# Block attention and routed experts on one core: another order of the steps of every attention pair

## The chip, the core and the metric

The kernel runs on one core of a Trainium2 chip. The metric is the device time of one execution in microseconds (us). It was timed three times before the change, and once more under the hardware profiler.

## What is computed

Eight batches of eight heads attend over 576 positions of width 64 with a mask by blocks of 64. The 4608 resulting rows of 512 then go through a layer of eight experts, each row through the one expert that its router picks.

```python
scores = scale * np.matmul(q, k.transpose(0, 1, 3, 2))          # (8, 8, 576, 576)
scores = np.where(block_i >= block_j, scores, -1000000000.0)
attn = np.exp(scores - np.max(scores, axis=-1, keepdims=True))
attn = attn / (np.sum(attn, axis=-1, keepdims=True) + 1e-09)
x = np.matmul(attn, v).transpose(0, 2, 1, 3).reshape(4608, 512)
...
logits = xn @ en.T / tau                                        # 8 experts
expert_idx = np.argmax(logits, axis=1)
...
    h = np.maximum(x[mask] @ w1[e], 0.0)
    out[mask] = gate_w[mask, None] * (h @ w2[e])
```

## The kernel before

Attention goes first, in 32 pairs of heads (four pairs to a batch), then the experts' layer in slots of 128 rows. The change touches the attention alone.

The work on a pair is cut into steps, Python generators that issue a few instructions and yield. Pass `n` of the loop over pairs (line 739) draws from five of them, which belong to different pairs, so that the engines always have work of several kinds:

- `s`, `scores` (line 377), pair n, ten steps, five to a head. TensorE (PE) forms a transposed tile of scores by two products (L384, L385) in one of two PSUM buffers `pss`; ScalarE (ACT) takes the exponential (L394, L401); GpSimd (POOL) adds tiles up for the sums of a row (L375). The second product reads `qx`, in which one row is the negated maxima of the pair.
- `v`, `values` (line 406), pair n-1, nine steps. Steps 1 to 6 are the products of the probabilities with v (L414): the two heads go to the two halves of PE's columns, in tiles of 128 by 64. Step 7 forms the sums with a matrix of ones (L423, L424, L428) in tiles of 128 by 32. Steps 8 and 9 copy sums and products out of PSUM, on VectorE (DVE, L430) and on ACT (L432). All of it lies in the one buffer `psb`.
- `f`, `post` and `finish` (line 437), pair n-1, four steps after the values: two of PE (L452, L456), turning the products into `psb` again, and two of DVE (L460 to L473), which read `psb` and divide.
- `m`, `maxes` (line 345), pair n+1, eleven steps: ten products of q and k on PE (L353), each in one of two buffers `psm` that DVE reduces to maxima (L355), then a turn of the maxima on PE (L360), a copy on ACT (L362), and two small DMAs (L364) that put them into `qx`.
- `p`, `prep` (line 297), pair n+2, six steps: turns of q (step 1) and of k (step 4) on PE (L312), copies on ACT (L324, L328, L333), the low parts by subtraction on DVE (L303, steps 2, 3, 5 and 6), a DMA of `qx` (L326) and four of `ka` (L336).

Two more letters stand in a plan. `l` loads q, k and v of pair n+3 (seven DMAs, L204 to L212; in pass 29 the first weights, L160). `r` draws one step of the router of the batch before (line 509): small DVE operations, six products for the ranks of its rows in `psm` (L538 to L542), the squares on ACT (L504), the store of the rows, and five scatters by indirect DMA on POOL (L604). Behind the last `r` of the batch before the last come the reading of a table (L630, a DMA of SyncE) and of the first rows for the experts (L499).

All DMAs but the scatters and gathers are issued by SyncE (SP), in the program's order. Every engine works its instructions in the order in which the program issues them, and waits by semaphores where an operand is not ready. So the order within a pass is set by one string of letters: eight of them stand in `PLANS` (line 21), number 0 to 7 here. Pass n takes plan n mod 4, the last four passes (28 to 31) plans 4 to 7; pass 0 has a plan of its own. A generator that is not drawn to its end by the string is drawn to it at the end of the pass.

```python
        for c in PLANS[n % NP + (NP if n >= NPAIR - NP else 0)] if n else PLAN0:   # line 744
            if c == "l":
                ...
            elif c != "r":
                parts[c] = drain(parts[c], 1)
            if c == "r" and slow and drain(slow[0], 1) is None:
                slow.pop(0)
```

Of the kernel before, what the change touches and what calls it, by code (L numbers as in the profile page):

```python
# [18 lines left out]


PLANS = (
    "vvrmmsvvmmsrrvrrpmsrmvvvsvmrmrsrsprmrrmrlpffssrrmrfmfrrpspsp",
    "vvmrrmrvrrvvrsmmrsvpsmrmvvsvmmspsmrfprmlfsmrfsfppprrssm",
    "rvvmmvvvrmrrmrrsrpvsrrsrmmvslvmvmpssmmfrrfrpffmssppmspsrrr",
    "vvvrmrrsrrrsrmrvrrrrrmmprrvsmmrrvvrsrrrvvmmrrrsspmmfrfrrmpslsprrrfrrrfrppssm",
    "vvvrsmmrvrrrvvrrmmrvvrrrrrssrmrlrrrmvrpsmrsmmrpfsrrrpfmrsfmmrsfpsrprprrs",
    "vvrvrrrmrrpmsrsrmpvvsrmlrrsrvvsvvrmrrsrmmrrrrfrrmsmpmfrmsffprmprrssp",
    "vvrrrrmrvvprvrrlmrsrvrrmsmrrrspvvmsspmvrrpsmfprrmmrsfrmmrsrrrsfpmrrsrfrrr",
    "mvrrvvprssvvpvmsrlrsmrrmrrmrrrvrvssvrssfmrfmmrprprmmpmpsfsfrm",
)  # L30
PLAN0 = "kmsmsmmsmmkpsmsspkmmmpmslsspspp"

# [1361 lines left out]
```

## Time and profile before

| | us |
|---|---|
| median of three runs | 895.87 (895.05 to 896.83) |
| the profiled execution, its own time | 888.07 |
| its span, from the first to the last instruction | 886.2 |
| end of the last exponential of pass 31, from the start of the span | 423.85 |

Attention takes the first half of the span, with passes of 12.4 to 12.7 us in the middle; the experts' layer takes the second half. A time in the rows below counts from the start of the span. A PE row names the stationary operand's tile (128*128, 128*64), and its end is modelled; the start of one product and of the next one tell how long PE was taken up by it.

### The profile page before, as it was taken

The page shows a single profiled execution, that of the slowest core. Times are in us where ns is not written, and L with a number is a line of the kernel's source. Part 1 is how long each engine was busy: PE and PEld are TensorE (multiplying, and loading weights), DVE is VectorE, ACT ScalarE, POOL GpSimd, SP SyncE. Part 2 cuts the span into 40 slices and gives each one's busy share as a digit, 9 for nine tenths or more (in the row PEclk, how much of TensorE's full clock was granted, in tenths as well). Part 3 has the DMA queues.
Part 4 walks back from the last instruction along what each step waited for, and adds up shares of the span by engine and source line. Part 5 has one row for each costly group of instructions (what it writes and reads, how often), then busy time and mean ns, then how long its engine had stood idle before and what let it go on. Part 6 is the DMA issues. An engine that isn't in the chain of part 4 may idle for free. (4 is left out here: it accounts for less than half of the span.)

```text
span 886.2 us, 18968 instructions
## 1 busy us (share of the span) xinstructions
PE 856.8 (97%) x5149; PEld 675.4 (76%) x5149; DVE 589.5 (67%) x1297; ACT 482.5 (54%) x959; POOL 522.0 (59%) x657
## 2 busy tenths in 40 slices
PE   5999999999999999998899999999899999999997
PEld 4777777777777777765687888888688888888885
DVE  8678888788888888784767534544667544566442
ACT  4655768576675767574745444645445333444331
POOL 6444664656555664648645322335688887687863
PEclk8899999999999999999999999999999999999999
DMA  8967877777887888774529443554676554354441
GB/s 157 190 153 148 172 179 162 171 152 169 170 188 149 165 185 162 165 190 139 190 79 301 140 144 130 172 208 164 215 242 205 187 171 155 119 159 140 151 134 48
DMA packets 172330, 146.67 MB, mean 166 GB/s; under 512 B 132009, under 2 KB 141449, under 8 KB 170652
## 3 DMA queue, kind: packets, MB, share of 16 engines
q1 hardware_dynamic: 150668, 100.14, 47.0%
q0 software_dynamic: 14896, 32.89, 12.3%
q10 hardware_dynamic: 6624, 12.06, 3.7%
q8 instruction: 51, 0.84, 0.4%
q14 instruction: 91, 0.75, 0.3%
HBM read 85.12 MB, written 31.79 MB: 132 GB/s over the span
## 5 line engine op out<-in xcount | busy, mean ns | idle before, releaser
L355 DVE TENSOR_REDUCE nmx<-psm 128x1 f32<-128x320 f32 x315 | 135.0, 452 | 46.3 <-PE psm L353 41.8
L394 ACT ACTIVATE pT<-pss 128x448 f32<-128x448 f32 (+1 forms) x254 | 112.6, 452 | 93.6 <-PE pss L385 88.7
L375 POOL TENSOR_TENSOR pS<-pT 128x448 f32<-128x448 f32 x64 | 72.9, 1139 | 128.7 <-ACT pT L394 128.7
L375 POOL TENSOR_TENSOR pS<-pS,pT 128x320 f32<-128x320 f32 (+2 forms) x192 | 115.6, 602 | 23.8 <-ACT pT L401 7.5
L384 PE MATMUL pss<-qb,ka 128*128 128x448 f32 (+1 forms) x382 | 126.4, 343 | 0.5 <-ACT pT L394 0.3
L1020 PE MATMUL py<-ring_h,hh 128*128 (+1 forms) x288 | 114.1, 396 | 2.6 <-ACT hh L964 2.3
L414 PE MATMUL psb<-pT,vo 128*64 128x448 f32 (+4 forms) x768 | 111.8, 408 | 1.7 <-DVE lgh L473 1.2
L1020 PE MATMUL py<-ring_h,hl 128*128 (+1 forms) x288 | 113.1, 393 | 0.2 <-DVE hl L962 0.2
L1020 PE MATMUL py<-ring_l,hh 128*128 (+1 forms) x288 | 112.7, 391 | 0.0
L385 PE MATMUL pss<-qx,kx 70*128 70x448 f32 (+1 forms) x382 | 109.3, 309 | 2.8 <-DMA qx<-nmT 2.8
L1020 PE MATMUL ph<-ring_h,xl 128*128 x280 | 109.3, 390 | 1.0 <-DVE xl L1013 1.0
L1020 PE MATMUL ph<-ring_h,xh 128*128 x280 | 110.0, 393 | 0.0
L1020 PE MATMUL ph<-ring_l,xh 128*128 x280 | 109.1, 390 | 0.0
L788 DVE TENSOR_TENSOR ring_l<-raw,ring_h 128x1024 f32 (+1 forms) x64 | 81.2, 1279 | 26.4 <-ACT ring_h L784 19.4
L1069 POOL DMA_INDIRECT out_dram<-y,outi x36 | 40.3, 1118 | 93.9 <-ACT y L1066 80.5
L353 PE MATMUL psm<-kd,qd 128*128 128x320 f32 x315 | 89.6, 347 | 3.1 <-ACT kd L333 1.8
L384 PEld LDWEIGHTS pss<-qb,ka 128*128 128x128 f32 x382 | 73.4, 192 | 21.6 <-issue 6.3
L1066 ACT ACTIVATE y<-py,gate 128x512 f32<-128x512 f32 x36 | 24.8, 689 | 116.8 <-PE py L1020 95.0
L353 PEld LDWEIGHTS psm<-kd,qd 128*128 128x128 f32 x315 | 55.5, 194 | 37.0 <-ACT pT L401 13.4
L1038 ACT ACTIVATE h<-ph 128x512 f32<-128x512 f32 x70 | 41.7, 598 | 76.7 <-PE ph L1020 69.0
L385 PEld LDWEIGHTS pss<-qx,kx 70*128 70x128 f32 x382 | 73.8, 193 | 4.0 <-DMA qx<-nmT 1.8
L784 ACT CAST ring_h<-raw 128x1024 f32 (+1 forms) x68 | 70.3, 1053 | 7.5 <-ACTq L929 4.2
(270 smaller groups left out, 1785.6 us busy)
## 6 DMA issues: line engine op xcount, KB each, us to landing
raw<-in_moe_w_dram SPq DMA_DIRECT2D x40, 512.0 KB
ka<-kd SPq DMA_DIRECT2D x128, 144.0 KB
raw<-in_moe_w_dram SPq DMA_DIRECT2D x12, 1024.0 KB
hrows<-h ACTq DMA_DIRECT2D x46, 256.0 KB
hq<-hrows POOLq DMA_DIRECT2D x92, 128.0 KB, 2.8
qn<-in_q_dram SPq DMA_DIRECT2D x64, 144.0 KB
kn<-in_k_dram SPq DMA_DIRECT2D x64, 144.0 KB
qx<-qb SPq DMA_DIRECT2D x32, 288.0 KB
```

What stands on the lines that cost most here:

```text
L353: nc.tensor.matmul(mx[:, 0:max(e - a, 256)], qd[d][:, j, :, :], kd[d][:, a:a + max(e - a, 256)], start=True, stop=True)
L355: nc.vector.tensor_reduce(m[:, j + u:j + u + 1], mx[:, 0:e - a], axis=AX.X, op=ALU.max, negate=True)
L375: nc.gpsimd.tensor_tensor(o, pT[0:r, P:S] if t == 1 else o, pT[0:r, off[t]:off[t] + w], op=ALU.add)
L384: nc.tensor.matmul(o, ka[i][:, hh, ts], qb[i][:, hh, c0:c1], start=True, stop=False)
L385: nc.tensor.matmul(o, kx[i][0:KX, hh, ts], qx[i][0:KX, hh, c0:c1], start=False, stop=True)
L394: nc.scalar.activation(pT[:, o:o + c1 - c0], st[:, 0:c1 - c0], AF.Exp, scale=scale)
L414: nc.tensor.matmul(ob[hh * D:(hh + 1) * D, c0:c1], a[:, t, hh, :], pTs[hh][0][:, o:o + c1 - c0], start=(t == 0), stop=(c0 == OB or t == NJ ...
L784: return nc.scalar.copy(piece(ring_h, to, c, half), raw[i][:, c * CW:(c + 1) * CW])
L788: return eng.tensor_tensor(piece(ring_l, to, c, half), raw[i][:, c * CW:(c + 1) * CW], piece(ring_h, to, c, half).bitcast(F32), op=ALU.sub ...
L1020: m = nc.tensor.matmul(out, a[:, c, :], w, start=(c == 0 and w is wh and a is sh), stop=(c == nk - 1 and a is sl_))
L1038: nc.scalar.activation(h[:, f:f + 512], ph, AF.Relu)
L1069: nc.gpsimd.indirect_dma_start(out=out, out_offset=bass.IndirectOffsetOnAxis(ap=to, axis=0), in_=y, in_offset=None, bounds_check=NT - 1, o ...
```

## The change

The eight strings of `PLANS` are replaced; nothing else. All letters but `r` stand in each new string as often as in the old one (`v` nine times, `s` ten, `m` twelve, `p` six, `f` four, `l` once); of `r` there are 18, 13, 16 and 34 in plans 0 to 3 before and 58, 11, 17 and 19 now, and 30, 26, 31 and 19 in plans 4 to 7 before and 34, 29, 24 and 19 now. The two most different of the first four:

```diff
 PLANS = (
-    "vvrmmsvvmmsrrvrrpmsrmvvvsvmrmrsrsprmrrmrlpffssrrmrfmfrrpspsp",
...
-    "rvvmmvvvrmrrmrrsrpvrsrrsrmmvslvmvmpssmmfrrfrpffmssppmspsrrr",
...
+    "vvvvvvlsrrmrmvvvrrrrrmrrsmsrpmrrsrrrrrrrmprrfmrrprrsmrrsrrrrffrmsrrrrsprrmrrrrrsrsrrrmrrrrrrmrrrfrpp",
...
+    "rrrmmrvrrrvrrvvrvrvvsrvvmmsplsmsmpfmmssprfmmrrffsspmmpssrrp",
...
 )
```

On PE, in a pass with plan 2, from the first product of the values on. Before:

```order
L414 MATMUL psb<-pT,vo_170 64x128 x2
L414 MATMUL psb<-pT,vo_170 64x448 x2
L353 MATMUL psm<-kd_200,qd_198 128x320
L353 MATMUL psm<-kd_200,qd_198 128x256
L414 MATMUL psb<-pT,vo_170 64x448 x2
L414 MATMUL psb<-pT,vo_170 64x320 x2
L414 MATMUL psb<-pT,vo_170 64x192 x2
L353 MATMUL psm<-kd_200,qd_198 128x512
L353 MATMUL psm<-kd_200,qd_198 128x448
L384 MATMUL pss<-qb_187,ka_193 128x288
L385 MATMUL pss<-qx_190,kx_196 128x288
L312 MATMUL pst<-ident,qn 128x96 x6
```

And now, at the same place:

```order
L353 MATMUL psm<-kd_200,qd_198 128x320
L353 MATMUL psm<-kd_200,qd_198 128x256
L414 MATMUL psb<-pT,vo_170 64x128 x2
L414 MATMUL psb<-pT,vo_170 64x448 x4
L414 MATMUL psb<-pT,vo_170 64x320 x2
L414 MATMUL psb<-pT,vo_170 64x192 x2
L414 MATMUL psb<-pT,vo_170 64x64 x2
L423 MATMUL psb<-pT,ones 32x128
L424 MATMUL psb<-pS,ones 32x320
```

The products of the values (L414) and of the sums (L423 to L428) stood in four pieces in this pass, with maxima, scores and turns between them; now they stand in one, with the first two products of the maxima ahead of it. A piece is counted from the first of these products to the next product of another kind. Over the whole attention there were 123 pieces and there are now 50: 4 for each of the values of pairs 0 to 26 before and 2, 1, 1, 2 in turn now (108 and 40 in all), and 15 and 10 for those of pairs 27 to 31.

On SP, in a pass with plan 2, up to the stores that follow it (`qx<-nmT` are the maxima, `ka<-kd` the turned k). Before:

```order
L326 DMA qx_190<-qb_187 64x1152
L364 DMA qx_189<-nmT 1x9x64 x2
L336 DMA ka_193<-kd_199 64x576 x4
L492 DMA xbuf<-xrow 64x256
L493 DMA xbuf<-xrow 128x4x256
```

and now:

```order
L326 DMA qx_190<-qb_187 64x1152
L336 DMA ka_193<-kd_199 64x576 x4
L364 DMA qx_189<-nmT 1x9x64 x2
L492 DMA xbuf<-xrow 64x256
L493 DMA xbuf<-xrow 128x4x256
```

The two DMAs of the maxima stood ahead of the four of `ka`, and stand behind them now. This is so in plans 0, 1 and 2; in plan 3 the maxima still go first.

On POOL, in pass 30, between the additions of pass 29 and the gather of the first rows. Before:

```order
L604 DMA table<-tokf,rowj 36864x1 x3
L375 TENSOR_TENSOR pS<-pT 128x448
L375 TENSOR_TENSOR pS<-pS,pT 128x320
L375 TENSOR_TENSOR pS<-pS,pT 128x192
L375 TENSOR_TENSOR pS<-pS,pT 64x64
L604 DMA table<-tokf,rowj 36864x1 x2
```

and now:

```order
L580 TENSOR_TENSOR ss<-ss,half 128x5
L604 DMA table<-tokf,rowj 36864x1 x5
L375 TENSOR_TENSOR pS<-pT 128x448
L375 TENSOR_TENSOR pS<-pS,pT 128x320
L375 TENSOR_TENSOR pS<-pS,pT 128x192
L375 TENSOR_TENSOR pS<-pS,pT 64x64
```

The last two scatters stood behind the additions of the pass's first head; now all five stand ahead of them. The reading of the table on SP (L630), which waits for the last scatter, stands ahead of the two DMAs of the maxima of pass 30 in both orders.

## Rows read from the trace of the kernel before

**Rows 1.** The page of the profile: the span, and the busy time of the engines over it.
```profile
span 886.2 us, 18968 instructions
PE 856.8 (97%) x5149; PEld 675.4 (76%) x5149; DVE 589.5 (67%) x1297; ACT 482.5 (54%) x959; POOL 522.0 (59%) x657
```

**Rows 2.** Busy time by stretch, passes 16, 17 and 18 of the loop over pairs one by one, then passes 20 to 23 together, then passes 28 to 31 together (a pass ends with its last exponential). Columns: start and end, length, and for PE, PE weight loads (PEld), DVE, ACT and POOL the busy time with the number of instructions; then the granted clock, the share of DMA time and GB/s.
```profile
219.05:231.53 12.48, 12.48 (x100) 9.23 (x96) 9.53 (x25) 7.67 (x17) 8.01 (x12) 1.00 1.00 198
231.53:244.00 12.47, 12.47 (x104) 9.58 (x102) 11.15 (x35) 7.79 (x18) 5.85 (x9) 1.00 0.72 145
244.00:256.37 12.37, 12.28 (x98) 9.49 (x96) 10.86 (x34) 11.34 (x28) 7.07 (x10) 1.00 0.77 162
...
269.03:318.99 49.96, 49.88 (x392) 37.68 (x390) 41.97 (x121) 34.73 (x79) 29.58 (x40) 1.00 0.81 167
...
368.95:423.85 54.90, 50.23 (x352) 34.65 (x348) 33.98 (x105) 31.55 (x88) 35.72 (x51) 0.97 0.67 176
```

**Rows 3.** Waits of PE alone between 60 and 400 us, the two longest of the three that there are. Columns: who waited, for whom, us in total, times, the longest.
```profile
PE psm L560 <- DVE accb L555: 0.6, 1, 0.6
PE psm L360 <- DVE nmx L355: 0.5, 1, 0.5
```

**Rows 4.** The timeline of PE in passes 17 to 19 (start us, duration us, line, tiles, shape, how many in a row). L414 is a product of the values, L384 and L385 one of the scores, L353 one of the row maxima, L312 a turn of q or k, L360 the turn of the maxima.
```profile
234.22 0.40 PE L384 MATMUL pss<-qb,ka 128*128 128x288 f32 x1
234.46 0.30 PE L385 MATMUL pss<-qx,kx 70*128 70x288 f32 x1
234.59 0.60 PE L353 MATMUL psm<-kd,qd 128*128 128x512 f32 x2
235.03 0.29 PE L384 MATMUL pss<-qb,ka 128*128 128x288 f32 x1
235.16 0.29 PE L385 MATMUL pss<-qx,kx 70*128 70x288 f32 x1
235.39 0.34 PE L414 MATMUL psb<-pT,vo 128*64 128x64 f32 x4
...
243.43 1.19 PE L414 MATMUL psb<-pT,vo 128*64 128x128 f32 x8
244.55 0.53 PE L353 MATMUL psm<-kd,qd 128*128 128x320 f32 x2
245.01 1.84 PE L414 MATMUL psb<-pT,vo 128*64 128x448 f32 x12
246.77 0.70 PE L353 MATMUL psm<-kd,qd 128*128 128x512 f32 x2
...
253.60 0.27 PE L360 MATMUL psm<-ident,nmx 128*9 128x128 f32 x1
255.95 1.94 PE L414 MATMUL psb<-pT,vo 128*64 128x128 f32 x12
257.82 0.41 PE L353 MATMUL psm<-kd,qd 128*128 128x320 f32 x1
258.20 0.30 PE L385 MATMUL pss<-qx,kx 70*128 70x288 f32 x1
...
258.81 0.76 PE L414 MATMUL psb<-pT,vo 128*64 128x320 f32 x4
259.50 0.70 PE L353 MATMUL psm<-kd,qd 128*128 128x512 f32 x2
...
260.63 0.55 PE L414 MATMUL psb<-pT,vo 128*64 128x192 f32 x4
261.11 0.47 PE L384 MATMUL pss<-qb,ka 128*128 128x448 f32 x1
```

**Rows 5.** The timeline of DVE in pass 14, from the last row maxima to the end of the division by the sums (L460 to L473).
```profile
202.57 0.42 DVE L355 TENSOR_REDUCE nmx<-psm 128x1 f32<-128x128 f32 x2
...
204.15 0.16 DVE L460 TENSOR_SCALAR rin<-psb 128x2 f32<-128x2 f32 x1
...
205.81 0.75 DVE L303 TENSOR_TENSOR kx<-pst,kd 64x576 fp32r<-64x576 f32 x1
```

**Rows 6.** SyncE's own timeline in pass 18: when it issued DMAs (start us, time that the issuing took, line, destination and source, how many).
```profile
254.19 1.58 SPq L364 DMA_DIRECT2D qx<-nmT  x2
255.88 2.69 SPq L336 DMA_DIRECT2D ka<-kd  x4
```

**Rows 7.** DMA issues of line L336 over the whole run: nanoseconds of one issue, least, median and most.
```profile
L336 SPq DMA_DIRECT2D ka<-kd x128: 469/587/2927, 8.2 to 399.3; - x128
```

**Rows 8.** Groups of instructions of ACT in passes 16 to 27, shapes kept apart: line, operation, tiles, shape, count, then busy us and mean ns of one, then the idle time before.
```profile
L333 ACT CAST kd<-pst 128x576 fp32r<-128x576 f32 x12 | 7.7, 640 | 0.0
```

**Rows 9.** The timeline of all engines at the end of pass 30 and the start of pass 31, by engine; what stands in brackets is how long the engine sat idle before, and what ended it.
```profile
408.50 0.26 ACT L362 CAST nmT<-psm 9x128 fp32r<-9x128 f32 x1 [0.79 <-PE psm L360]
...
411.62 0.34 SPq L630 DMA_DIRECT2D et<-table  x1
...
412.07 1.59 SPq L364 DMA_DIRECT2D qx<-nmT  x2
...
413.95 0.40 PE L385 MATMUL pss<-qx,kx 70*128 70x288 f32 x1 [1.59 <-DMA qx<-nmT]
```

**Rows 10.** Busy time by stretch at the same place, columns as in rows 2.
```profile
410.60:414.00 3.40, 1.81 (x10) 0.52 (x6) 0.00 (x0) 1.88 (x10) 3.08 (x6) 1.00 0.03 1
414.00:417.00 3.00, 3.00 (x16) 1.95 (x17) 0.00 (x0) 0.71 (x2) 1.80 (x5) 0.60 0.56 156
```

More of the change, by code (lines that the diff above doesn't have):

```diff
@@ L21 @@
 PLANS = (
-    "vvrmmsvvmmsrrvrrpmsrmvvvsvmrmrsrsprmrrmrlpffssrrmrfmfrrpspsp",
[L23 to L29, printed above, removed]
+    "vvvvvvlsrrmrmvvvrrrrrmrrsmsrpmrrsrrrrrrrmprrfmrrprrsmrrsrrrrffrmsrrrrsprrmrrrrrsrsrrrmrrrrrrmrrrfrpp",
+    "rrvvvrrvvvlmmvvvmmssprmsrmrsfpmmsfspmmsrpssrfrmrfppms",
+    "rrrmmrvrrrvrrvvrvrvvsrvvmmsplsmsmpfmmssprfmmrrffsspmmpssrrp",
+    "mmvvvvrvvvrrrvrvmrmssrprmrrlrrssrmrfprmmssrfpmmssrfmfppprrssm",
+    "vrvvvrmrmssmrrrrprmrsrrmsrvrvrvrprpvmsrslrvrrrmpmrrsmrsrppmrrrffssrrmrfrmrrf",
+    "prrmmvvrpvvrvprvmsrmvvsrvmrmsprsmlsrrrmsrrsfprrrrrrrsmmfrsmsfrmrrfprrrr",
+    "mmpppvvprrvvvvrvrrrssrvrmrppvlrrrrmrssmfrmmsrsmfrmrrmsrrsmsrfrrmfs",
+    "vvvvvrrrmrrssmrpvrrmmsrsrrprplmrvsmsvvmpmpprssrfrfmsmsrrmmrff",
 )
```

## The prediction

> **What bounds the kernel now.** I read the busy times by stretch first. In the middle of attention PE is busy in all but 0.08 us of 49.96 that four passes take, at the full clock; DVE is busy for 41.97 of them and ACT for 34.73 [rows 2]. The waits of PE say the same: from 60 to 400 us the longest two are 0.6 and 0.5 us in all [rows 3]. So from pass 1 to 27 PE never stands still, and a pass can become shorter only if PE's own work becomes shorter. The page's 97% for PE alone would not tell this [rows 1], since it also holds the experts' half.
>
> Next I read the timeline of PE, by the starts of its products [rows 4]. The same product takes more of PE's time when it stands beside a piece of the values' products. A second score product holds PE for 0.13 us ahead of an ordinary product (234.46 to 234.59) and for 0.23 ahead of a piece (235.16 to 235.39): entering costs 0.10. The first score product behind a piece holds it for 0.24 (234.22 to 234.46) and an ordinary one for 0.13 (235.03 to 235.16): 0.11. Within the pieces, steps 1 to 3 in one took 1.87 (255.95 to 257.82) and steps 1 and 2 took 1.12 (243.43 to 244.55), so step 3 inside a piece is 0.75. Steps 3 to 5 in one took 1.76 (245.01 to 246.77), so steps 4 and 5 inside one are 1.01. In pieces of their own they took 0.69 and 0.48 (258.81 to 259.50, 260.63 to 261.11), 0.16 more for the one piece more. So a piece costs 0.10 + 0.11 + 0.16 = **0.37 us** of PE. The tile of the stationary operand changes there, 128*128 to 128*64 and back.
>
> **The change, part by part.** Values' steps. The values of pairs 0 to 26 go from 108 pieces to 40: 68 x 0.37 = 25.2 us less of PE. Those of pairs 27 to 31 go from 15 to 10: 1.9 less. The amount of arithmetic is the same. Four passes of 49.96 would come down by 10 x 0.37 to 46.3.
>
> The Trainium skill ("TensorEngine Tiling", Key Properties) says that changing the tiling mode drains TensorE, and ("TensorE: Matmul & The Clock Gate", Single matmul latency) gives a warm product a fixed part of 398 cycles at 2.4 GHz. An estimate from that page is 0.17 us for each change and 0.33 for a piece; 73 pieces would then give 24.2 us instead of the 27.1 by the rows, which I keep.
>
> Cover. DVE, ACT and POOL hid under PE's 49.96; they must now fit 46.3. DVE has 4.3 us to spare in four passes instead of 8.0, ACT 11.6 [rows 2]. What matters is when: during the one long piece, some 3.4 us (2.88 for steps 1 to 5, and I take 0.5 for 6 and 7), PE makes no maxima for DVE and no scores for ACT. DVE has the low parts of k left over for it, two of about 0.75 [rows 5], and router steps; the squares of the router fall into it on ACT in plan 2 (ACT has 11.34 us of work in that pass, 7.79 in the one before [rows 2]). For the rest of the pass both have to run nearly without a break. Three places can hold PE up:
>
> 1. The first product of the values writes `psb`, which the last division of the pass before reads. In plan 0 that step (`f`, fourth) now comes nearly last. DVE needs 1.66 us for the division (204.15 to 205.81) and 0.42 for the last two maxima between [rows 5], some 2.1; PE has four score steps and a turn ahead of the values, 2.35 us in pass 18 (253.60 to 255.95 [rows 4]). I take 0.1 us a pass.
> 2. Scores in plans 1 and 2: two buffers `pss`, and ACT's 7.8 us a pass almost all behind the values' piece, in a pass of 11.6 less 3.4. I take 0.1.
> 3. The maxima's DMA. It now stands behind the four of `ka` on SP in three plans of four. From the turn of k: 0.64 us for ACT's copy [rows 8], 4 x 0.587 for the issues [rows 7], 1.88 from the issue to the reading product (412.07 to 413.95, where PE waited for it [rows 9]), 0.1 for the handing over: 5.0. PE has about 1.2 of scores, 3.4 of values and 0.9 of maxima in that time, 5.5. Before, the issue stood 4.01 us ahead of the reader (254.19 [rows 6] to 258.20 [rows 4]), 2.1 to spare; 0.5 are left. I take 0.05.
>
> So 0.25 us a pass, 6.8 over 27 passes, are given back. The bounds are 0 (everything fits) and 0.65 (the first rival).
>
> The router's ranks. On PE they stand ahead of the turn of the maxima now instead of ahead of a product of maxima, and on DVE the reading follows the first half of the division instead of a low part. Neither was waited for before [rows 3] in the steady passes. Nothing gained, and at most 0.2 us in each of seven batches lost: within the range. The steps with no work left that plan 0 draws cost nothing.
>
> The loads (`l`) come right behind the values' sixth step in plans 0 and 1, and SP then waits for PE's reading of v; PE gets there early in the pass, and what stands behind is needed a pass later. Nothing. The DMA share, already 1.00 in pass 16 [rows 2], rises by 8%, and covers the bytes only because all but the maxima are wanted a pass ahead.
>
> The end of attention. In pass 30 the maxima were turned and copied by 408.76, but SP stood at L630 until the last scatter had landed, and issued them at 412.07; PE waited until 413.95 [rows 9], was busy for 1.81 us of 3.40, and then ran at half the clock for most of the next stretch (granted 0.60 [rows 10]). With all five scatters ahead of the additions on POOL the last one comes earlier by the four additions, and SP is free when the maxima come. At best the whole wait and the slow clock go: 1.9 + 1.5. At the other end nothing is gained, since other waits follow closely. I take 2.0.
>
> The experts' half moves as a whole and is costed at nothing; it would be late only if attention's end stopped being what starts it.
>
> **Sum.** -25.2 - 1.9 + 6.8 - 2.0 = -22.3 us. The profiled execution's 888.07 (span 886.2) becomes 865.8. The median of the runs, 895.87, stands 7.8 above that execution; taken from it the forecast is **873.6 us**.
>
> **Rivals.** *DVE becomes the bound.* For it: 41.97 of 46.3 busy, and an idle stretch of about 1.5 us in every long piece (3.4 less 1.5 of low parts and little else). Four passes then take 41.97 + 6 to 6.5, about 48.3: 1.7 less than now, 11 over the 27 passes, plus 1 or 2 at the end: 883.5. Against it: leftovers may be kept in the queue, up to two maxima, two low parts and the router's steps. The Trainium skill ("TensorEngine Tiling", PSUM Bottleneck) warns of this: a faster TensorE leaves the emptying of PSUM as the bottleneck. By that rule the gain is the 11 to 13 us of this rival.
>
> *The maxima come late, and it is slower.* If DMAs ahead on the rings delay the landing of the maxima, PE stops at L385 in three passes of four, some 20 times. The reserve is 0.5 us; to eat up the 27.1 gained it takes stops of 1.35 us, a landing 1.9 later than reckoned. At stops of 1.6 us, 32 in all, the median would be 901. For it: an issue of `ka` has taken up to 2.9 us [rows 7], and 1.88 was seen with the DMAs idle (share 0.03 [rows 10]). Against it: four `ka` issues took 2.69 us in pass 18 [rows 6], little over the median.
>
> *The price of a piece is not real.* PE's ends are modelled; if the starts moved without cost, or the gaps are filled by waits that were hidden, the time stays at 895 to 897. Against it: the 49.96 is the sum of just these starts.
>
> **How the numbers follow.** About 0.2%, 1.8 us, can be told from no change here. The forecast's case (a gain of 15 to 30 us) has 0.70, the DVE rival 0.18, the one without effect 0.05, the slower one 0.07. Faster by over 0.2% is then 0.88, within it 0.05, slower by over 0.2% 0.07. The range starts at everything fitting and the end's wait gone, 895.87 - 27.1 - 3.4 = 865.4, taken as 866, and ends a little above the DVE rival, 886.
>
> **What would show it.** Right: passes of about 11.8 us, one or two pieces of L414 in each, PE still busy in nearly all of it, DVE busy about 89% of the middle, no wait at L385 in pass 31 and no half clock behind it. Wrong: rows of PE or its weight loads waiting for DVE's reductions or division (the DVE rival), for the DMA of the maxima (the slower one), or passes of 12.4 with fewer pieces (no effect).

## The result: 0.6% slower instead of 2.5% faster

The changed kernel takes 898.91 us (median; 895.0 to 904.75) against 893.72 (890.76 to 896.83) for the kernel before, measured together: 1.006 times, 95% interval 1.0043 to 1.0078. Forecast were 873.6 us with a range of 866 to 886; the time lies outside it, on the side of the rival with a chance of 0.07. The profiled execution of the changed kernel took 903.12 us, so the two traces (901.4 and 886.2 us of span) lie 15 us apart where the medians lie 5: the profiled execution of the kernel before, 888.07 us, was shorter than any of its twenty timed runs. The traces say where, the ratio how much.

The page of the changed kernel, span and PE, answers to [rows 1]: as many products, 6 us less of busy time, and a longer span.

```profile
span 901.4 us, 19001 instructions
PE 850.6 (94%) x5149; PEld 685.9 (76%) x5149; DVE 583.1 (65%) x1297; ACT 477.0 (53%) x959; POOL 521.2 (58%) x657
```

Passes 4 to 27 take 306.3 us (70.45 to 376.75); before they took 299.8 (69.12 to 368.95). Busy time of some of them, the changed kernel, columns as in [rows 2]: pass 4; pass 8 (plan 0) and two pieces of it; passes 17, 18 and 19; passes 28 to 31; and a piece of pass 31.

```profile
70.45:82.23 11.78, 11.54 (x98) 9.43 (x96) 9.18 (x25) 7.46 (x17) 5.79 (x8) 1.00 0.85 172
...
119.07:134.17 15.10, 13.38 (x98) 10.89 (x96) 9.19 (x25) 7.70 (x17) 9.80 (x12) 0.89 0.83 157
121.28:123.35 2.07, 0.40 (x5) 0.21 (x2) 0.00 (x0) 0.00 (x0) 1.60 (x3) 1.00 0.63 127
125.00:127.00 2.00, 2.00 (x8) 1.67 (x8) 1.55 (x4) 0.98 (x3) 0.00 (x0) 0.50 0.98 197
...
237.29:249.86 12.57, 12.29 (x104) 9.77 (x102) 11.20 (x35) 7.61 (x19) 5.83 (x10) 1.00 0.74 152
249.86:261.80 11.94, 11.83 (x100) 9.69 (x100) 10.41 (x34) 10.98 (x27) 7.21 (x11) 1.00 0.69 142
261.80:274.04 12.24, 12.11 (x102) 9.53 (x99) 10.40 (x30) 7.70 (x19) 6.83 (x9) 1.00 0.80 200
...
376.75:436.20 59.45, 50.94 (x352) 37.78 (x348) 33.45 (x106) 31.71 (x88) 38.58 (x53) 0.91 0.59 157
421.00:425.00 4.00, 4.00 (x16) 1.56 (x14) 0.00 (x0) 2.04 (x11) 2.86 (x9) 0.50 0.53 145
```

Plan 0 takes 11.78 us in pass 4 and 15.10 in pass 8, with the same 98 products on PE. The passes with plan 0 from 8 to 24 take 71.95 us in all, where five of 12.48 took 62.4: 9.55 lost. The other nineteen passes take 234.35 instead of 237.4: 3.1 won. The last four passes take 59.45 instead of 54.90; the first four take 1.3 us more, and what follows the loop 2.9. PE's busy time is shorter than before, so the longer span is waiting. The waits of the changed kernel that bear on it (60 to 375 us; who waited, for whom, us, times, the longest):

```profile
PE pss L385 <- DMA qx<-nmT: 9.5, 9, 2.1
PEld pss L384 <- ACT pT L401: 6.4, 20, 0.5
PEld pss L385 <- DMA qx<-nmT: 6.0, 5, 1.8
PEld pss L384 <- ACT pT L394: 3.2, 11, 0.4
PEld pss L384 <- ACT qd L328: 1.4, 3, 0.5
```

The first line is the maxima's DMA, and new beside [rows 3]; the third is the weight loads of the same products, so that most of it is the same time seen twice. Of PE's 9.5 us, 7.8 fall at the start of the five long passes with plan 0. In two passes a stop cost more than itself, since the clock fell behind it. In pass 8 PE was busy for 0.40 of the 2.07 us from 121.28, and from 125 to 127 the granted clock was 0.50, its lower level. The 98 products kept PE busy for 13.38 us there, and for 11.81 to 12.32 in passes 12, 16 and 20 at the full clock, so 1.1 to 1.6 us of pass 8 go with the clock. Pass 24, the other with a granted 0.89, is alike (13.28 busy, 15.56 long). The weight loads' waits for ACT, three lines, are not larger than before: there three such lines hold 12.7, 3.7 and 3.1 us in the same stretch, and PE itself waited for ACT in none of it.

One such wait for the maxima, on PE's timeline at the start of pass 8, with the maxima's turn and copy ahead of it, and SP's timeline (the step that answers to [rows 6]):

```profile
117.01 0.27 PE L360 MATMUL psm<-ident,nmx 128*9 128x128 f32 x1
117.65 0.24 ACT L362 CAST nmT<-psm 9x128 fp32r<-9x128 f32 x1
118.70 2.65 PE L414 MATMUL psb<-pT,vo 128*64 128x448 f32 x20
121.28 0.40 PE L384 MATMUL pss<-qb,ka 128*128 128x288 f32 x1
123.35 0.37 PE L385 MATMUL pss<-qx,kx 70*128 70x288 f32 x1 [1.68 <-DMA qx<-nmT]
```

```profile
108.53 1.58 SPq L364 DMA_DIRECT2D qx<-nmT  x2
110.22 0.51 SPq L492 DMA_DIRECT2D xbuf<-xrow  x1
...
114.47 0.57 SPq L493 DMA_DIRECT2D gbuf<-xrow  x1
115.14 1.06 SPq L204 DMA_DIRECT2D qn<-in_q_dram  x2
...
117.40 1.00 SPq L211 DMA_DIRECT2D vo<-in_v_dram  x2
...
119.27 0.56 SPq L326 DMA_DIRECT2D qx<-qb  x1
119.92 1.60 SPq L364 DMA_DIRECT2D qx<-nmT  x2
```

The same place in the kernel before:

```profile
116.36 0.27 PE L360 MATMUL psm<-ident,nmx 128*9 128x128 f32 x1
117.05 1.57 SPq L364 DMA_DIRECT2D qx<-nmT  x2
119.00 0.90 SPq L204 DMA_DIRECT2D qn<-in_q_dram  x2
120.15 0.29 PE L385 MATMUL pss<-qx,kx 70*128 70x288 f32 x1
```

The maxima of pair 8 are turned at 117.01 (L360) and lie ready from 117.89, the end of ACT's copy. SP takes until 119.92 to come to them: six stores, seven loads and one copy stand ahead, fourteen issues in 9.7 us and nearly without a gap. The reader starts 3.43 us after the issue. In the kernel before the same transfer left SP at 117.05, 0.69 behind its turn, and 3.10 ahead of its reader; in pass 18 it was 4.01 [rows 4, 6]. There the loads of plan 3 were issued behind the maxima (119.00); the change also put these loads ahead. Pass 4 has two stores ahead instead of six, and no wait: its maxima leave 0.48 us after they are ready.

### The profile page after: what moved, and what is told of

Its sections match the earlier page's. It is cut to its first block, busy times and chain, and to the rows that moved or that the text cites. A ratio compares the mean times of both kernels' runs of the same rounds, so it can differ in the third digit from the quotient of the medians.

```text
span 901.4 us, 19001 instructions
## 1 busy us (share of the span) xinstructions
PE 850.6 (94%) x5149; PEld 685.9 (76%) x5149; DVE 583.1 (65%) x1297; ACT 477.0 (53%) x959; POOL 521.2 (58%) x657
## 3 DMA queue, kind: packets, MB, share of 16 engines
q0 software_dynamic: 14896, 32.89, 12.2%
## 5 line engine op out<-in xcount | busy, mean ns | idle before, releaser
L394 ACT ACTIVATE pT<-pss 128x448 f32<-128x448 f32 (+1 forms) x254 | 108.9, 452 | 72.3 <-PE pss L385 57.5
L384 PE MATMUL pss<-qb,ka 128*128 128x448 f32 (+1 forms) x382 | 121.7, 331 | 6.4 <-ACT pT L394 2.7
L385 PE MATMUL pss<-qx,kx 70*128 70x448 f32 (+1 forms) x382 | 110.8, 316 | 16.2 <-DMA qx<-nmT 15.0
L353 PE MATMUL psm<-kd,qd 128*128 128x320 f32 x315 | 99.4, 366 | 4.5 <-DVE nmx L355 1.8
L414 PE MATMUL psb<-pT,vo 128*64 128x448 f32 (+4 forms) x768 | 97.3, 402 | 1.6 <-DVE lgh L473 1.6
L384 PEld LDWEIGHTS pss<-qb,ka 128*128 128x128 f32 x382 | 74.7, 195 | 21.9 <-ACT pT L394 7.2
L385 PEld LDWEIGHTS pss<-qx,kx 70*128 70x128 f32 x382 | 74.7, 195 | 20.7 <-issue 9.0
L414 PEld LDWEIGHTS psb<-pT,vo 128*64 128x64 f32 x768 | 51.5, 140 | 45.6 <-issue 32.7
```

The costliest lines, as they stand in the source:

```text
L353: nc.tensor.matmul(mx[:, 0:max(e - a, 256)], qd[d][:, j, :, :], kd[d][:, a:a + max(e - a, 256)], start=True, stop=True)
L384: nc.tensor.matmul(o, ka[i][:, hh, ts], qb[i][:, hh, c0:c1], start=True, stop=False)
L385: nc.tensor.matmul(o, kx[i][0:KX, hh, ts], qx[i][0:KX, hh, c0:c1], start=False, stop=True)
L394: nc.scalar.activation(pT[:, o:o + c1 - c0], st[:, 0:c1 - c0], AF.Exp, scale=scale)
L414: nc.tensor.matmul(ob[hh * D:(hh + 1) * D, c0:c1], a[:, t, hh, :], pTs[hh][0][:, o:o + c1 - c0], start=(t == 0), stop=(c0 == OB or t == NJ ...
```

## Experiments

**Theory A:** the new order puts the maxima's transfer behind other issues on SP, and these waits take back what the fewer pieces gain. **B:** the transfers are late because too much is in flight. **C:** ACT has no room behind the long piece. All ratios are to the kernel before, run beside them.

**Middle or end.** Plans 0 to 3 new and 4 to 7 old, and the other way round.

```
PLANS = new[:4] + old[4:]     # new_steady
PLANS = old[:4] + new[4:]     # new_end
```

> New plans 0 to 3, old plans 4 to 7. The trace after has two losses: passes 4 to 27 took 306.3 us against 299.8, passes 28 to 31 took 59.5 against 54.9. Theory 1 (the middle decides: the maxima's DMAs late on SyncE, and ScalarE out of step): most of the 5 us stays, 896 to 899. Rival (the end decides: the five scatters and the table's reading at the end of attention): about 0 to +1, 893 to 895, or a gain if the middle is faster in most executions.

> Old plans 0 to 3, new plans 4 to 7: the other half. Theory 1: +1 to +3, 895 to 897. Rival (the end decides): the whole +5, 898 to 900. If the two halves are independent, the changes of this run and of the one before add up to that of all eight plans.

Measured: 901.95 us, 1.0111 (1.0088 to 1.0134), and 890.87, 0.9992 (0.9972 to 1.0013). The loss is the middle's. The end alone gives nothing. Both times miss what Theory 1 expected (896 to 899, and 1 to 3 us lost), and the halves do not add up: 1.0111 with the new middle alone against 1.006 with all eight plans, so by these ratios the new end is worth some 0.5% behind the new middle. In the trace with the new middle and the old end, passes 28 to 31 take 58.90 us, nearly the 59.45 of the changed kernel.

**Loads behind the maxima, plan 3.**

```
-mmvvvvrvvvrrrvrvmrmssrprmrrlrrssrmrfprmmssrfpmmssrfmfppprrssm
+mmvvvvrvvvrrrvrvmrmssrprmrrrrssrmrfprmmssrfpmmssrfmlfppprrssm
```

> All new plans, but in plan 3 the letter l (seven DMAs of loads) stands behind the eleventh m (the maxima's DMAs) instead of ahead of it. Theory 1: the waits of PE at L385 at the start of passes with plan 0 (1.3 to 2.5 us each, some 12 us, and up to 2 us more where the clock fell behind one) go, the rest stays: 884 to 889, passes with plan 0 at 11.8. Rival (ScalarE or VectorE pace these passes anyway, the wait only hides it): the wait goes but the passes stay at 13 to 15, 897 to 900.

Measured: 906.64 us, 1.0181 (1.0152 to 1.021): worse, where 884 to 889 were expected. Plan 0's passes are cured (12.51 us in pass 8), but plan 1's take 14.3 to 18.6. SP shows why: the loads of plan 3 now meet those at the head of plan 0, the keys stand behind both, and the next maxima (L360 at 137.87) leave at 142.01.

```profile
130.55 2.47 SPq L336 DMA_DIRECT2D ka<-kd  x4
133.12 1.14 SPq L204 DMA_DIRECT2D qn<-in_q_dram  x2
...
138.99 2.92 SPq L336 DMA_DIRECT2D ka<-kd  x4
142.01 1.59 SPq L364 DMA_DIRECT2D qx<-nmT  x2
```

**Stores on another queue.** In `store`, `nc.sync.dma_start` became `nc.gpsimd.dma_start`, in the changed kernel and in the one before; or `nc.scalar.dma_start` in the changed one.

> The changed kernel with the row blocks' stores (L492, L493: six transfers in every fourth pass) issued by POOL instead of SP; all else as changed. In the changed kernel the maxima's transfer of plan 0's passes left SP up to 2.9 us behind the product that made the maxima, behind six stores and seven loads; of its seven plan 0 passes only pass 4, which has no stores ahead, took 11.78 us, the six others 13.20 to 15.56. Theory A (SP's queue is what makes the maxima late): with the stores off SP the waits at L385 in plan 0's passes shrink from 1.0 to 2.5 us to under 0.3, plan 0's passes take 11.8 to 12.3 us, and the whole is about 14 us shorter than the changed kernel: ratio to before 0.988 to 0.993. Rival B (the transfers themselves are late because the 16 DMA engines are full, share 1.03 around the longest stall; it does not matter who issues them): the transfer leaves SP earlier but lands as late as now, plan 0's passes stay above 13 us, ratio 1.002 to 1.008. Rival C (POOL has to issue them between its additions, and the sums wait): ratio above 1.008 with new waits on POOL.

> The same, with the stores issued by ACT. Theory A: the waits at L385 in plan 0's passes go as with POOL, less what six issues of some 0.55 us (what they take on SP) cost ACT, 3.3 us in every fourth pass, partly in the 4 us that ACT idles behind the sums' copy: plan 0's passes 11.8 to 14 us, ratio 0.988 to 1.000. Rival B: plan 0's passes stay above 13 us and gain nothing, ratio 1.002 to 1.015.

> The kernel before with the stores issued by POOL. Theory A: before, the maxima's transfer has room on SP in every plan (no wait at L385 in its passes 4 to 27), so nothing changes: ratio 0.997 to 1.003. Rival: SP's queue also costs the order before something, ratio below 0.997; then a gain of the changed kernel with POOL's stores is not owed to the change alone.

Measured: 896.44 us, 1.001 (0.9972 to 1.0048) with POOL; 921.52, 1.0328 (1.0308 to 1.0348) with ACT; 899.81, 1.0082 (1.0054 to 1.011) for the kernel before with POOL. With POOL, plan 0's passes fall to about 12.5 as A says, but passes 11 and 15 now wait up to 3.31 us at L385: A's number is missed. While POOL stores, SP's own issues are slow (two loads of v in 3.03 us from 113.01, against 1.00 above), which is of B's kind; what slows them is not shown. On ACT the maxima are late again: in pass 7 ACT's copy of them ends at 108.09, ahead of its stores, but SP issues them at 113.05, behind four keys (done at 111.14) and a wait of 1.8 us for the landing of a store. PE waits for them 22.3 us in all. Stores issued by POOL cost the kernel before 0.8% too, where none was expected.

**The piece's price.** A step of the maxima put inside the values' piece, in plans 1 to 3.

```
-rrvvvrrvvvlmm...     -rrrmmvrrrv...     -mmvvvvr...
+rrvmvvrrvvvlm...     +rrrmrvmrrrv...     +mvvmvvr...
```

> The changed kernel with one piece of values' products more in each pass with plan 1, 2 and 3 (a step of the maxima put between the first and second step of the values; in plan 3 two), all other steps in their order. Theory of the piece's price (0.37 us on PE each): passes with plan 1 take 12.9, with plan 2 12.3, with plan 3 12.6 us (changed kernel: 12.57, 11.95, 12.25 where no wait at L385 stands), the whole about 7 us longer than the changed kernel. Rival (PE waits for ACT in these passes, so a piece more costs nothing): the passes stay within 0.1 us.

Passes 17, 18 and 19 (plans 1, 2, 3) of that kernel:

```profile
240.96:253.88 12.92, 12.64 (x105) 9.90 (x103) 11.21 (x35) 7.60 (x19) 5.80 (x10) 1.00 0.72 148
253.88:266.17 12.29, 12.21 (x102) 9.79 (x100) 10.85 (x34) 10.99 (x28) 7.18 (x11) 1.00 0.68 138
266.17:278.45 12.28, 12.17 (x101) 9.48 (x99) 10.47 (x30) 7.68 (x18) 6.82 (x9) 1.00 0.81 200
```

Plans 1 and 2 take 0.35 us longer each than above; there the piece's price is real, 0.35 against 0.37 reckoned. Plan 3 shows only 0.04, and why is not shown. The one run took 906.05 us, 7.1 over the changed kernel's median; passes 4 to 27 take 310.1 in its trace, 3.8 more than the changed kernel's. The prediction's estimate of 0.33, worked out from the Trainium skill ("TensorE: Matmul & The Clock Gate", Single matmul latency), agrees with 0.35 too.

**No wait for the maxima.** The transfer L364 left out from the fourth pair on; the scores use stale maxima.

```
-for hh in range(2):                     # L363
+for hh in range(2 if n < NBUF else 0):
```

> The changed kernel with the maxima's transfer (L364) left out from the fourth pair on, so that the scores take the maxima of an earlier pair and wait for none. Theory A: no wait at L385, passes 11.8, 12.6, 11.95, 12.25 us throughout, no fall of TensorE's clock in the middle, passes 4 to 27 take 291 to 293 us (changed kernel 306.3, before 299.8), the whole 878 to 886 us. Rival B (something else makes plan 0's passes long): plan 0's passes still 13 us and more.

Measured: 886.61 us in one run, 12.3 under the changed kernel; passes 4 to 27 take 295.6:

```profile
70.83:366.43 295.60, 289.31 (x2342) 231.20 (x2340) 247.28 (x721) 203.17 (x475) 174.11 (x230) 1.00 0.79 169
```

Plan 0 takes 12.5 to 12.7 us from pass 8 on and no more 13 to 15.6, and the granted clock is 1.00. So the lateness is the loss. But 295.6 is over the 291 to 293 expected: a second thing holds PE.

**ACT's room.** The copies L328 on POOL, and then left out from the third pair on (stale maxima again).

```
-(... else nc.scalar.copy)(               # qd_pool, L328
+(... else nc.gpsimd.tensor_copy)(
-for hh in range(2):                      # no_qd, L327
+for hh in range(2 if n < 2 else 0):
```

> All new plans, and the two copies of q's high part (L328, 1.36 us a pass on ScalarE) on GpSimd instead. Theory 2 (ScalarE stands idle in the long piece of the values and then sets the pace, so that score products wait for a free buffer): the time between a product of maxima of 256 columns and the score product behind it falls from 1.95 us too much in four passes to under 1, passes with plan 1 from 12.57 to 12.0 or less, 885 to 891 in all. Rival (VectorE sets the pace): plan 1 stays at 12.5, 897 to 900; a second way to lose is GpSimd, which would then be late with the additions for the sums: PE waiting for it at L424.

> The changed kernel with the copies of the queries into the blocks of the maxima's operand (L328, on ACT 0.67 us each, two in a pass) left out from the third pair on, so that the maxima are those of earlier queries. Theory of ACT's room (after the long piece the scores wait for ACT, 0.7 us a pass that the prediction had at 0.1): passes with plan 1, 2 and 3 that have no wait at L385 fall by 0.3 to 0.7 us, from 12.57, 11.95 and 12.25. Rival (the score waits are not ACT's, or POOL's additions and DVE's steps take their place): within 0.1 us of these, as plan 1's rose with the copies on POOL.

On POOL: 897.14 us, 1.0073 (1.0053 to 1.0093), no gain where 885 to 891 were expected: plans 2 and 3 take 11.67 and 12.08 us in passes 18 and 19, plan 1 loses 0.5. Left out (894.63 us, one run), passes 17, 18, 19:

```profile
232.71:245.15 12.44, 12.28 (x106) 9.90 (x104) 11.43 (x35) 6.51 (x18) 5.83 (x10) 1.00 0.74 153
245.15:256.68 11.53, 11.38 (x96) 9.37 (x94) 10.01 (x34) 9.88 (x25) 7.21 (x11) 1.00 0.72 148
256.68:268.58 11.90, 11.74 (x100) 9.55 (x102) 10.54 (x31) 6.62 (x17) 6.84 (x9) 1.00 0.78 199
```

Plans 1, 2 and 3 fall by 0.13, 0.41 and 0.34 us here; over all six passes plan 1 does not fall (75.35 us against 75.48). ACT's work is on the path in plans 2 and 3, hardly in plan 1.

**The whole key step behind the maxima**, and the loads of plans 0 and 3 later.

```
plans 0 to 2: fourth p behind the eleventh m;  plan 0: l behind the second p;  plan 3: l behind the eleventh m
```

> The changed kernel with the maxima's transfer (L364) put ahead on SP's queue in every plan 0 to 3: the step of the keys' transfers ka (L336) in plans 0, 1 and 2, and the loads of plan 3, moved behind the step that makes the maxima, and the loads of plan 0 moved from its head to behind its second step of preparing. In the changed kernel L364 leaves SP 2.4 to 3.4 us behind L360 in every plan, before it 0.6 to 2.5, and what is left between issue and first use is 2.2 us against 3.1 to 4.5 before. Theory A (the changed order lets the maxima's transfer stand behind other issues on SP, and that wait takes the gain back): L364 leaves SP within 1 us of L360 in plans 1, 2 and 3 and within 2 in plan 0, the waits at L385 fall from 15 us to under 3, passes take 11.8, 12.6, 11.95 and 12.25 us and the ratio is 0.985 to 0.992. Rival B (the transfer lands late because of what is in flight, not of what is issued ahead; as with the stores on POOL, where it took 3.6 to 4.4 us from issue to use): the waits stay above 8 us and the ratio is 1.000 to 1.008. Rival C (what is put behind is late in its turn, as with the loads behind the maxima alone: 1.018): new waits at L312 or L384 for loads or keys, ratio above 1.008.

Measured: 898.64 us, 1.0053 (1.0033 to 1.0073). The waits at L385 are gone, as A says, but plan 1 takes 13.62 us and plan 2 12.30. The ratio is that of neither A nor C; of C's kind is that something put behind is late in its turn, though not at L312 or L384. The step holds the keys' six turns and ACT's copy too, and DVE's low parts wait for it, 13.9 us against 1.9 in the changed kernel. That this is what lengthens the passes is argued, not tested.

**SP alone.** The keys' issues are kept back until the maxima's are out, the loads moved as above; all else in the changed order.

```
+def keys(i=i, d=d, hd=hd):
     for hh in range(2): ...              # the four L336
+if n < 3 or made[0] >= n - 1: keys()
+else: kaq.append(keys)
...                                       # in maxes, behind L364
+made[0] = n
+while kaq: kaq.pop(0)()
```

> The changed kernel with SP's queue alone reordered: the keys' transfers (L336) are issued behind the maxima's (L364) of the same pass in every plan, the loads of plan 3 behind the maxima's, the loads of plan 0 behind its second step of preparing; PE, DVE, ACT and POOL keep the changed kernel's order step by step. Theory A (place on SP's queue is all that makes the maxima late): waits at L385 in the middle under 2 us in all, passes 12.5 (plan 0), 12.58, 11.95 and 12.2 to 12.4 us as with the maxima's transfer left out, passes 4 to 27 take 295 to 297 us (before 299.8, changed 306.3), ratio 0.990 to 0.995. Rival (with the steps where they were, keys or loads land late, or the transfer still takes over 3 us to land): waits at L384, L312 or L385 of over 5 us in all, ratio 0.998 to 1.008.

Measured: **877.31 us, 0.9863 (0.9842 to 0.9884)**, faster than both kernels. SP, PE and passes 16 to 19 and 28 to 31 of it (L371 is the maxima's DMA, L339 the keys', L395 the waiting score):

```profile
115.75 1.57 SPq L371 DMA_DIRECT2D qx<-nmT  x2
...
121.62 2.47 SPq L339 DMA_DIRECT2D ka<-kd  x4
```

```profile
114.84 0.27 PE L367 MATMUL psm<-ident,nmx 128*9 128x128 f32 x1
...
119.34 0.30 PE L395 MATMUL pss<-qx,kx 70*128 70x288 f32 x1
```

```profile
213.81:225.71 11.90, 11.69 (x98) 9.41 (x96) 9.17 (x25) 7.46 (x17) 9.79 (x12) 1.00 0.87 174
225.71:238.29 12.58, 12.29 (x104) 9.79 (x102) 11.22 (x35) 7.61 (x20) 5.83 (x10) 1.00 0.83 171
238.29:250.23 11.94, 11.83 (x100) 9.69 (x100) 10.40 (x34) 10.98 (x27) 7.19 (x11) 1.00 0.86 173
250.23:262.12 11.89, 11.79 (x101) 9.50 (x99) 10.46 (x30) 7.69 (x19) 6.84 (x9) 1.00 0.69 176
359.11:408.64 49.53, 46.04 (x352) 34.57 (x348) 33.16 (x105) 31.78 (x88) 33.43 (x47) 1.00 0.74 190
```

The maxima leave 0.91 us behind their turn, and 3.59 ahead of the reader, which does not wait. Passes 4 to 27 take 290.8 us. That is better than A's numbers (295 to 297, ratio 0.990 to 0.995), and 4.8 better than with no transfer to wait for at all. So A's cause is confirmed, and something beside it is won: plan 3 takes 11.89 us and plan 0 11.9, where 12.2 to 12.4 and 12.5 were expected. The last experiment comes back to this.

**Its parts, and the same on the kernel before.** The keys' issues alone, the loads alone, the keys' issues in the old order.

```
ka_late: keys() kept back, new plans as changed     loads_moved: l moved, keys() at once
ka_late_before: keys() kept back, old plans
```

> The changed kernel with the keys' transfers alone issued behind the maxima's; the loads stay where the change has them (plan 3's ahead of the maxima's transfer, plan 0's at its head). Theory A: the small waits of plans 1 and 2 go, but plan 0's passes keep their waits at L385 of 1 us and more, since stores and loads stand ahead there: plan 0 takes 13 to 15 us, ratio 1.000 to 1.005. Rival: the keys' transfers are the whole cause, plan 0 at 12 us and ratio under 0.992.

> The changed kernel with the loads alone moved (plan 3's behind the maxima's transfer, plan 0's from its head to behind its second step of preparing); the keys' transfers stay ahead of the maxima's in plans 0 to 2. Theory A (both parts are needed, since SP is backed up from plan 3's loads through plan 0's keys): plan 0's own passes are cured (12 us), but the maxima's transfer of plan 0's pass now stands behind loads and keys, and plan 1's passes carry waits at L385 of 1 us and more; ratio 1.000 to 1.012. Rival: the loads are all of it, ratio under 0.990.

> The kernel before, its order of all steps kept, with the keys' transfers (L336) issued on SP behind the maxima's (L364) of the same pass. Theory A: before, PE waits for no maxima in passes 4 to 27, so nothing is to be had there; passes stay at 12.48, 12.47, 12.37, 12.65 us, ratio 0.997 to 1.003, and the gain of the kernel with SP's queue reordered (0.986) belongs to the changed order once its transfers are in time. Rival: SP's order by itself is worth part of it, ratio under 0.996.

Measured: 895.17 us, 1.0063 (1.0045 to 1.0082); 902.54, 1.0129 (1.0108 to 1.0151); 889.07, 0.9991 (0.9978 to 1.0004). Each part alone leaves waits at the maxima's reader, 11.3 and 12.0 us between 60 and 375:

```profile
PE pss L395 <- DMA qx<-nmT: 11.3, 6, 2.8
```

```profile
PE pss L385 <- DMA qx<-nmT: 12.0, 8, 3.1
```

Only both together clear the queue, and in the old order there is nothing to clear. `ka_late` came a little over its expected 1.005, with plan 0 up to 17.2 us, and `loads_moved` over its 1.012.

**Two more on the best one:** the copies L328 on POOL in plans 2 and 3, and the old plans at the end.

```
sp_only_qd: ... else nc.gpsimd.tensor_copy if n % 4 < 2 and n > 3 else nc.scalar.copy
sp_only_old_end: PLANS[4:] = old[4:]
```

> The same, and in plans 2 and 3 the two copies of the queries (L328) go to POOL. Leaving them out took 0.42 us from plan 2's passes and 0.35 from plan 3's; on POOL in all plans they took 0.25 and 0.2 there and cost plan 1 0.5 us. Theory of ACT's room: plan 2 takes 11.7 and plan 3 12.0 us, plan 1 and 0 as in the kernel with SP's queue alone reordered; 3 us less than that one, ratio 0.987 to 0.992. Rival (POOL's additions come later and the sums of the next pass wait): what plans 2 and 3 gain, plans 0 and 1 lose, no difference between the two kernels.

> The kernel with SP's queue alone reordered, with the old plans 4 to 7 in the last four passes. Theory (the end's term, 3.9 us by the prediction, is real once the stalls are gone: those passes took 49.5 us in the kernel with SP reordered, 54.9 before): passes 28 to 31 take 53 to 56 us, ratio 0.990 to 0.994. Rival (the end's gain is the middle's, which leaves it less to wait for): passes 28 to 31 as short as with the new plans, ratio 0.985 to 0.988.

Measured: 881.21 us, 0.9899 (0.9879 to 0.9919): plan 2 falls to 11.53, but plan 0 rises to 13.10, where the sums (L434) wait for POOL's additions, 6.8 us of weight-load waits between 60 and 375. The rival's mechanism held, and plan 0 loses more than plans 2 and 3 gain: the ratio is within the theory's 0.987 to 0.992, but 0.4% above the kernel without the copies on POOL. With the old end: 887.7, 0.9948 (0.9933 to 0.9962); passes 28 to 31 take 54.19 us instead of 49.53, so the new plans of the end are worth 4.7 there. The rest of the difference is in the middle, where plans 3 and 0 took 12.4 and 12.5 us in the traced execution and not 11.9, with the same order of steps. The traces show where this begins in plan 3. In pass 19 of the two kernels (first SP alone, then with the old end) PE starts its products at the same times from the pass's start, up to and beyond the last ones of the sums (L438), but DVE's copy of the sums (L440) follows the last of them 0.42 us later in one and 0.95 in the other:

```profile
253.27 0.34 PE L438 MATMUL psb<-pS,ones 128*32 128x192 f32 x2
253.70 0.49 DVE L440 COPY su<-psb 97x320 f32<-97x320 f32 x1 [0.28 <-PE psb L438]
```

```profile
258.31 0.34 PE L438 MATMUL psb<-pS,ones 128*32 128x192 f32 x2
259.27 0.49 DVE L440 COPY su<-psb 97x320 f32<-97x320 f32 x1 [0.80 <-PE psm L360]
```

What follows on DVE and ACT is as much later. This delay is 0.42 in every middle pass with plan 3 of the kernel with SP alone reordered, and 0.70 to 0.95 in those of the kernel without the maxima's transfer; why is open.

## Why the prediction was wrong, step by step

- **PE bounds it, and a piece costs 0.37 us: right in two plans of the three tried.** A piece added costs 0.35 there. Ten pieces fewer in four passes are 3.5 us.
- **Place 3, the maxima's transfer behind the keys: this failed.** I reckoned with four key issues, an idle landing of 1.88 us [rows 9] and 0.5 us in reserve, and took 0.05 us a pass. I did not count what else stands on SP: the six stores and the loads of plan 3. The loads I took at "Nothing", since what stands behind them is needed a pass later, and looked at plans 0 and 1; in plan 3, where the maxima go ahead of the keys, they now stand behind the loads. There the maxima waited 2.0 us for SP after they were ready, and from issue to reader took 1.5 us more than idle. The 0.05 a pass, 1.4 us in all, stood against 9.5 us of stops between 60 and 375 and the slow clock behind two of them. Without any wait for them the kernel is 12.3 us shorter, and with SP alone reordered the ratio goes from 1.006 to 0.986, part of which are the 0.5 us a pass in plans 3 and 0 that are open. The rival of late maxima named the mechanism and got 0.07; but it blamed the landing and the keys, in three passes of four, where 7.8 of the 9.5 us stand in plan 0's passes. That its 901 us is nearly the time is luck: it reckoned with 32 us of stops against 27.1 won.
- **Place 2, scores that wait for ACT: right in kind, too small.** In the kernel with SP reordered four passes take 48.31 us (213.81 to 262.12) instead of 49.96: 1.65 won of 3.5, so 0.46 a pass is given back, inside the bounds of 0 to 0.65 but not the 0.25 of the sum. Added up over the starts in these passes, a maxima's product ahead of a score holds PE 0.25 us (20 of them, 4.98), before 0.17 (10, 1.73). That ACT is behind it rests on the run without the copies L328, where plans 2 and 3 fall by 0.41 and 0.34 us; the weight loads' waits for ACT do not price it, being 19.5 us before, 11.0 in the changed kernel and 2.2 with these copies left out. In plan 1, where nothing fell, what holds PE is not shown. The Trainium skill ("TensorEngine Tiling", PSUM Bottleneck) warns, of a TensorE made four times as fast by tiling, that the copies out of PSUM may become the bottleneck; this case agrees in kind, though PE's work fell by only 3.5 us in 50, with ACT as the engine that empties PSUM.
- **Place 1 and the DVE rival: not seen.** In the kernel with SP reordered PE itself waits for no division (six weight loads do, 1.0 us in all), its weight loads wait 4.5 us for DVE's maxima between 60 and 375 against 10.8 for ACT, and DVE is busy 41.25 of these 48.31 us, 85%. The rival's own figure for four passes was 48.3; no run took work off DVE, so that it has no share in this is argued and not shown.
- **The end: the terms are real, but do not show in this kernel's trace.** The new plans of the end are worth 4.7 us with SP reordered, against 3.9 reckoned (1.9 for the pieces, 2.0 for the wait). In the changed kernel the four passes took 4.55 more than before, but not by the new end, since with the old one behind the new middle they take 58.90. What the trace shows there: SP comes to the weights' load of pass 29 behind the keys, at 401.56, 3.8 us ahead of the maxima (405.39), and L385 starts 1.60 us behind its L384, at 411.28 (with SP reordered the weights stand 9.5 us ahead, and it does not wait; the profile names no cause, so this is argued); PE waits 1.30 for DVE at 416.82, and the clock fell behind that, as in [rows 10]: 0.50 granted from 421 to 425, where twenty products of the values took 4.97 us, against 2.65 for twenty of nearly the same columns at 118.70. The wait of pass 31 itself did go: its reader ran at 425.79 behind the values, 6.0 us after the issue at 419.76.
- **The experts' half, costed at nothing: too little.** From the last exponential to the end of the span it took 462.31 us before, 465.22 in the changed kernel and 467.03 with SP reordered; why is open. With the queue in order 12.5 us are won (877.31 against 889.76) and not 22.3: by the traces passes 4 to 27 gave 9.0 where the sum had 16.4 for them, and this half took back 4.7.

## What to carry to other kernels

When steps are moved on the compute engines, list what the DMA-issuing engine does in the same span, all of it, stores and loads of other stages too, and lay each urgent transfer's ready time beside the time at which the queue comes to it. An order that is better for the busiest engine can be lost to a queue that no busy time shows; then reorder the queue alone before giving up the order. An engine kept without input by a long piece works off its share later, in the bound engine's way: cost that from its busy time in what is left of the pass.

## What the runs showed of the hardware

- In the stretch shown ahead of pass 8 most issues on SP took 0.5 to 0.8 us each, one of the maxima (1.60 for two) little more than a store (0.51) or a load (1.06 for two). One issue of the keys took up to 2.9 us elsewhere [rows 7].
- Behind stops of PE the granted clock fell to 0.50 in passes 8 and 31; the products of pass 8 kept PE busy for 13.38 us, the same ones at the full clock for 11.81 to 12.32.
- From issue to reader the maxima took 3.43 us in a loaded stretch (pass 8), 1.88 with the DMAs idle [rows 9].
- The same order of steps ran its plans 3 and 0 at 11.9 us a pass in one kernel and 12.4 to 12.5 in another that differs only in the last four passes. In plan 3 it begins with DVE's copy of the sums, 0.42 or 0.95 us behind the same product; what sets this is open.
